# Fold of a fused attention and mixture kernel in another order, and the late rows' transpose ahead of expert 1's traffic

## The chip, the core and the metric

The kernel runs on one core of one Trainium2 chip. TensorE (PE) multiplies, VectorE (DVE), ScalarE (ACT) and GpSimd (POOL) do the rest, and SyncE (SP) issues most of the DMAs. The metric is device time in microseconds (us) of one execution; the median of three runs of the kernel before is 903.72 us (902.86 to 906.01).

## The reference

Three stages follow one another, all in float32:

```python
# 1: linear attention with a decaying state, batch 4, 8 heads, 768 steps, 48 wide
for t in range(S):
    cur = einsum('bhd,bhe->bhde', u * k[t], v[t])
    y[t] = einsum('bhd,bhde->bhe', r[t], state + cur)
    state = w[t] * state + einsum('bhd,bhe->bhde', k[t], v[t])
# 2: a bilinear layer on 3072 tokens, d_model 384, d_ff 1024
x = ((x @ w1) * (x @ w2)) @ w3 @ w_out
# 3: eight experts, the two best of each token, weighted
logits = x @ w_gate + log1p(exp(x @ w_noise)) * noise
out[mask] += top2_w * (relu(x[mask] @ e1[e]) @ e2[e])
```

## The kernel before

**Numbers.** Every large product runs as three passes on TensorE (`mm3`, L179 to L182): an operand is a high part in the PE's own float32 format plus a low part, the remainder, and the passes are high by high, high by low, low by high. The parts are made by `split` (L136) or, for the weights that the host hands over as 64-bit words, by `cvt` and `flush` (L142 to L171): ACT pulls the top 16 bits out (`top`, L151), DVE joins them with the middle bits (`cvz`, L164), ACT casts the high part (L166), DVE subtracts for the low part (L171). The weights come in through DMAs on SP's queue into seven buffers `rawf`.

**Stages.** (1) *Fold*, up to about 66 us: the product w3 times w_out is formed on the chip, widened by 16 gate columns (w_out times w_gate and w_noise). Step `u` of the loop at L529 converts one piece of w_out (`cv_wo`, `u < 8`) and one of w3 (`cv_w3`, `u < 16`), multiplies the piece converted three steps before (`mm_w3`, 12 matmuls of 400 columns), turns the new w_out piece over on PE (`wo_T`, L397) and multiplies the turned piece of the step before with the gate weights (`gate_cols`, `gate_split`). After `wo_T`, ACT copies the turned piece out of PSUM (`woT`, L402). `warm_up` puts matmuls on a constant tile among these. (2) *Groups*, up to about 467 us: twelve groups of two chunks of 128 tokens; the attention of later chunks is spread among the products of earlier ones. (3) *Experts*, eight, each in two halves: four tiles of 128 rows, then two of 128 and one of 32. Rows are gathered by POOL (`gather`), stored by SP to a DRAM table (`store_first` for expert 0, `turn` for the others), and read back through a transposing DMA on SP (`turn_first`, `turn`) into `XTx`; `tr` splits `XTx` into `XTh` on ACT and `XTl` on DVE, `mm1` and `mm2` multiply. For expert 0 the last tiles' rows (tiles 5 and 6, the late rows) are known last.

**What sets the order.** DVE's instructions run in the order in which the code is written. PE and ACT are ordered by the tile scheduler, ACT and some of PE in program order where the code pins it (`act.on`, `keep_in_program_order`). SP and POOL work their DMAs off in order; an SP entry that waits holds all behind it. Within the fold, the steps that prepare attention chunks 0 to 2 (`STEPS`, L377), the loads of their inputs and the loads and conversions of w1 and w2 (quarters, `load_w`, `cv_w`) are hung at slots by tables (`WHEN`, `WLD`, `WCV`, `LDA`); step `u` runs at its end all that stands in slots `u - 24` to `u - 23`. `WHEN[j][i]` is the slot of step `i` of chunk `j`.

Of the kernel before, what the change touches and what calls it, by code (L numbers as in the profile page):

```python
# [20 lines left out]
DM, FF, E = 384, 1024, 8  # L21
# [50 lines left out]
def tile_kernel(ctx: ExitStack, tc: tile.TileContext, dt, nat, w3t, wout, w1, w2, e1, e2, cf, ci, out):  # L72
    nc = tc.nc
    pe, act, dve, pool, sp = nc.tensor, nc.scalar, nc.vector, nc.gpsimd, nc.sync
# [13 lines left out]
    act = Pinned()  # L88

    def f(ap):  # L90
        return ap.bitcast(F32)
# [7 lines left out]
    cft = const.tile([P, CFW], F32, name="cft")  # L99
    cit = const.tile([P, CIW], I32, name="cit")  # L100

    def c(n):
        o, w = CF[n]
        return cft[:, o:o + w]
# [16 lines left out]
    trib = const.tile([P, P], BF16, name="trib")  # L121
# [14 lines left out]
    def split(h, l, src, on=None):  # L136
        act.copy(out=h, in_=src)
        (on or dve).tensor_tensor(out=l, in0=src, in1=f(h), op=OP.subtract)
# [3 lines left out]
    def cvt(rw, n, h, l, o=0, post=None):  # L142

        t = TOP[0][:, :n]
        TOP.append(TOP.pop(0))
        top = rw.bitcast(BF16)[:, 4 * o + 4:4 * o + 4 * n + 4].rearrange("p (n t) -> p n t", t=4)[:, :, 0]
        mid = rw[:, 2 * o + 1:2 * o + 2 * n + 1].rearrange("p (n t) -> p n t", t=2)[:, :, 0]  # L150
        act.activation(out=t.bitcast(F16).rearrange("p (n t) -> p n t", t=2)[:, :, 1], in_=top, func=AF.Copy)  # L151
        z = cvp.tile([P, 512], I32, name="cvz")[:, :n]
        if post == "z":
            dve.scalar_tensor_tensor(z, mid, 13, t, op0=OP.logical_shift_right, op1=OP.bitwise_or)
            return z.bitcast(F32)
        flush(1)
        CQ.append((mid, t, z, h, l, post))

    def flush(n=2):
        for _ in range(n):  # L160
            low, LQ[:] = LQ[:], []
            while CQ:
                mid, t, z, h, l, post = CQ.pop()
                dve.scalar_tensor_tensor(z, mid, 13, t, op0=OP.logical_shift_right, op1=OP.bitwise_or)  # L164
                x = z.bitcast(F32)
                act.copy(out=h, in_=x)  # L166
                LQ.append((h, l, x))
                if post:
                    post(x)
            for h, l, x in low:  # L170
                dve.tensor_tensor(out=l, in0=x, in1=f(h), op=OP.subtract)  # L171

    def load64(rw, src):

        n = src.shape[-1]
        sp.dma_start(out=rw.bitcast(U16)[:, 1:4 * n + 1], in_=src.bitcast(U16))
        return rw[:, :2 * n + 2]
# [205 lines left out]
    rawx, w3s, xo_, R1 = {}, {}, {}, {}  # L383
# [3 lines left out]
    def ld_raw(n=1):  # L387
        for _ in range(n):
            if order:
                k, u = order.pop(0)  # L390
                rawx[k, u] = load64(raws.tile([P, 1026], I32, name="rawf"),
                                    wout[u] if k == "o" else w3t[u // 8, u % 8])

    def cv_wo(j):
        cvt(rawx["o", j], DM, woh[:, j, :DM], wol[:, j, :DM], post=lambda x: xo_.__setitem__(j, x))

    def wo_T(j):  # L397
        bank = PB[4 + j % 2]
        for kb in range(3):
            pe.transpose(bank[:, P * kb:P * kb + P], xo_[j][:, kb * P:kb * P + P], ident)  # L400
        xo_[j] = fold.tile([P, DM], F32, name="woT")
        act.copy(out=xo_[j], in_=bank[:, :DM])  # L402

    def gate_cols(j):
        g = bK[:, 256 + 32 * j:272 + 32 * j]
# [3 lines left out]
    def gate_split(j):  # L409
        split(woh[:, j, DM:], wol[:, j, DM:], bK[:, 256 + 32 * j:272 + 32 * j])  # L410

    def cv_w3(u):
        w3s[u] = [fold.tile([P, 512], F32R, name=x, bufs=3) for x in ("w3h", "w3l")]
        cvt(rawx["3", u], 512, *w3s[u])
# [17 lines left out]
    def piece(m, fp, i):  # L432
        r = R1[m, fp]
        return (r[i], 0) if isinstance(r, list) else (r, 384 * i)
# [4 lines left out]
        cvt(rw, 384, (WAh, WBh)[m][:, sl], (WAl, WBl)[m][:, sl], o)  # L439

    def cv_early():
        for i in range(2):
            rw, o = piece(1, 0, i)
            EZ.append(cvt(rw, 384, None, None, o, "z"))
# [16 lines left out]
    def at(slot, fn, *a):  # L461
        todo.setdefault(slot, []).append((fn, a))

    def run_todo(lo, hi):
        for slot in sorted(x for x in todo if lo <= x < hi):
            for fn, a in todo.pop(slot):
                fn(*a)

    WHEN = {0: (-13, -12, -14, -13, -14, -21, -18, -17, -17, -20, -19, -16, -14, 0),
# [5 lines left out]
    LATE = (6, 6, 0, 1, 1, -6, -4, -3, -2, -5, -3, -2, -1, -2)  # L475
    JT = 5
    WLD = {(0, 0): -16, (0, 1): -14, (1, 0): -13, (1, 1): -11, (0, 2): -8, (1, 2): -6, (0, 3): 1, (1, 3): 3}
    WCV = {(0, 0): -10, (0, 1): -9, (1, 1): -4, (0, 2): -1, (1, 2): 2.65, (0, 3): 4.1, (1, 3): 6.01}
    WSP = (-5, -2, 2.6, 2.61)
    LDA = (-24, -22, -20, -17, -18)  # L480

    at(-23, lambda: sp.dma_start(out=cft[:, ca:], in_=cf[:, ca:]))
    at(-20, lambda: pool.tensor_copy(out=trib, in_=c("tri")))
    for slot, fn, a in zip(LDA, (load_dt, load_na, load_dt, load_na), (0, 0, 1, 1)):
        at(slot, fn, a)
    at(LDA[4], lambda: sp.dma_start(out=cit, in_=ci))
    at(-8, cv_early)
    at(-5, cv_late)
    for fb in range(4):
        at(WSP[fb], split_w1, fb)  # L490
    for k, slot in WCV.items():
        for i in range(2):
            if slot != -9:
                at(slot, cv_w, *k, i)
    for k, slot in WLD.items():
        at(slot, load_w, *k)
    for i, fn in enumerate(STEPS):
        for j in range(NCH):
            late = 3 if j == NCH - 1 and i == 1 else 0
            at(WHEN[j][i] if j in WHEN else 6 * j - 14 + LATE[i] - late, fn, j)  # L500
    for i in range(2):
        at(-9, cv_w, 0, 1, i)
    at(-3, flush)
    at(-3, flush, 1)
    for slot in (0.1, 2.55, 2.9, 3, 5, 5.3, 6.02, 6.04):
        at(slot, flush, 1)

    ca = CF["u"][0]
    sp.dma_start(out=cft[:, :ca], in_=cf[:, :ca])
    ld_raw(6)  # L510
    warm = fold.tile([P, 512], BF16, name="warm", bufs=1)
    dve.memset(warm, 1.0)

    def warm_up(n):
        for _ in range(n):
            tc.keep_in_program_order(pe.matmul(PB[6], warm[:, :P], warm, start=True, stop=True))
# [12 lines left out]
    for u in range(19):  # L529
        if u < 8:  # L530
            cv_wo(u)
            ld_raw()
        if u < 16:
            cv_w3(u)
            ld_raw()
        elif u == 16:
            flush()
        if u > 2:
            mm_w3(u - 3)
        if 0 < u < 9:  # L540
            gate_cols(u - 1)
            gate_split(u - 1)
        if u < 8:
            wo_T(u)
        if u < 2:
            warm_up(3)
        act.on = u >= 15
        run_todo(u - 24, u - 23)

    flush()  # L550
    foldx.close()
# [223 lines left out]
    def load_e(e, m, i):  # L775
        if m == 0 and e:
            rw = EP["b"].tile([P, 1536], F32, name="raww", bufs=2)
        else:
            rw = rawp.tile([P, 1538], F32, name="raw2", tag="raw64")[:, :1536]
        RW[e, m, i] = rw  # L780
        tc.keep_in_program_order(sp.dma_start(out=rw, in_=(e1, e2)[m][e, :, 1536 * i:1536 * i + 1536]))
# [57 lines left out]
    def rows_of(j):  # L839
        return TPT if j < NT - 1 else TPL  # L840
# [10 lines left out]
    def turn(e, hf, mid=lambda: None):  # L851

        for j in range(TA) if hf == 0 else range(TA, NT):
            tc.keep_in_program_order(sp.dma_start(
                out=rows[e % 2, 2 * TPT * j:2 * TPT * j + 2 * rows_of(j)].rearrange("(p t) d -> p (t d)", t=2),
                in_=XG[e, j][:rows_of(j)]))
        mid()
        a = 2 * hf * NAB[0]
        s = slice(a, a + 2 * NAB[hf])
        tc.keep_in_program_order(sp.dma_start_transpose(out=XT["x", hf].bitcast(U16), in_=rows[e % 2, s]))  # L860
# [56 lines left out]
    def need(e, hf, r, rows=NROW):  # L917
        load_idx(e, hf, r)
        for j in range(TA) if hf == 0 else range(TA, NT):
            gather(e, j, rows)  # L920
# [54 lines left out]
    for g in range(NGRP):  # L975
# [10 lines left out]
        for i in range(12):  # L986
# [11 lines left out]
            k = SPG * g + i  # L998
# [47 lines left out]
    for j in range(TA):  # L1046
        mm2(0, j)
        if j == 0:
            need(1, 0, 0)
            for jj in (NT - 2, NT - 1):  # L1050
                store_first(jj)
            turn_first(NT - 2, CAP)
            load_e(1, 0, 0)
            load_e(1, 0, 1)
        if j == TA - 2:
            tr(0, 1)
    need(1, 1, 0)

    def load_w2():
        load_e(1, 1, 0)  # L1060
        load_e(1, 1, 1)

    for ff in range(8):
        mm1(1, ff)
    turn(1, 0)
    for i, j in enumerate((TA, NT - 1, *range(TA + 1, NT - 1))):
        mm2(0, j)
        split_e(1, 0, i)
# [132 lines left out]
```

## Time and profile before

| what | value |
|---|---|
| median of three runs | 903.72 us |
| the profiled execution, whole | 909.49 us |
| its span, first to last instruction | 907.7 us |
| PE busy | 882.4 us (97%) |
| DVE, ACT, POOL busy | 491.6, 436.3, 242.9 us |
| PE's share of the chain that ended last | 41%, DMA 1%, issue 2% |

A page of the profile lists busy time by engine, by slice of the span and by line; queries of the trace give the same for any stretch, list instructions in order of time with the idle time of the engine before each and what ended it, and sum who waited for whom. Times in them count from the span's start. Busy PE can hold inefficiency: a matmul's row lasts longer than the distance to the next one's start, because they are pipelined.

### The profile page before, as it was taken

Reading aid. Unit: us, or ns where it says so; the run is one execution under the profiler, and the core shown is the slowest. Engines: PE = TensorE matmul, PEld = TensorE weight load, DVE = VectorE, ACT = ScalarE, POOL = GpSimd, SP = SyncE. Lnnn points to the kernel's source line nnn. Section 1 sums busy time; section 2 is a strip of 40 time slices with the busy share of each in tenths; the row PEclk is TensorE's granted clock in tenths of the full one; section 3 lists DMA queues with packets and bytes.
Section 4 is the critical chain, followed back from the end, with each engine's and each line's share of the span. In section 5 each row is a group of like instructions: output and inputs, shape, how many; then the busy total and the mean of one; then the engine's idle time right before and its main releaser. Section 6 shows DMA issues by size and latency. Waiting matters only on the chain. (4 is left out here: it accounts for less than half of the span.)

```text
span 907.7 us, 17628 instructions
## 1 busy us (share of the span) xinstructions
PE 882.4 (97%) x7010; PEld 816.1 (90%) x7010; DVE 491.6 (54%) x1208; ACT 436.3 (48%) x883; POOL 242.9 (27%) x216
## 2 busy tenths in 40 slices
PE   8899999999999999999998999999999999999994
PEld 6789799999999999999988989899998989989894
DVE  5899766756666657655472453443434334353430
ACT  7787666555546547544552443433334343433320
POOL 1200010231231231132334443316061341603122
PEclk9999999999999999999999999999999999999997
DMA  9963479474575654515145986829276482934112
GB/s 352 409 232 129 130 99 262 130 196 142 144 216 139 178 134 128 146 44 167 36 114 108 256 249 173 204 73 222 62 214 143 133 213 65 229 76 108 18 21 38
DMA packets 123581, 139.18 MB, mean 153 GB/s; under 512 B 74592, under 2 KB 103264, under 8 KB 123488
## 3 DMA queue, kind: packets, MB, share of 16 engines
q1 hardware_dynamic: 99952, 109.58, 41.3%
q0 software_dynamic: 12160, 19.72, 11.2%
q10 hardware_dynamic: 11376, 8.65, 3.3%
q8 instruction: 57, 0.93, 0.4%
q14 instruction: 36, 0.29, 0.1%
HBM read 88.12 MB, written 36.04 MB: 137 GB/s over the span
## 5 line engine op out<-in xcount | busy, mean ns | idle before, releaser
L908 POOL DMA_INDIRECT out<-ye,ti x49 | 77.4, 1579 | 235.5 <-ACT ye L898 215.3
L180 PE MATMUL pb<-XTh,WAh 128*128 128x512 f32 (+1 forms) x384 | 134.2, 350 | 3.0 <-ACT XTh L865 2.3
L181 PE MATMUL pb<-XTl,WAh 128*128 128x512 f32 (+1 forms) x384 | 133.0, 347 | 0.0
L182 PE MATMUL pb<-XTh,WAl 128*128 128x512 f32 (+1 forms) x384 | 131.8, 347 | 0.0
L180 PE MATMUL pb<-WBh,HH 128*128 128x384 f32 x384 | 130.2, 339 | 0.0
L181 PE MATMUL pb<-WBl,HH 128*128 128x384 f32 x384 | 129.3, 337 | 0.0
L182 PE MATMUL pb<-WBh,HH 128*128 128x384 f32 x384 | 129.3, 337 | 0.0
L881 DVE SCALAR_TENSOR_TENSOR HH<-pb,HH 128x256 fp32r<-128x256 f32 (+1 forms) x128 | 71.3, 557 | 87.2 <-ACT HH L880 79.9
L880 ACT ACTIVATE HH<-pb 128x256 fp32r<-128x256 f32 (+1 forms) x128 | 62.8, 491 | 115.2 <-PE pb L182 108.2
L898 ACT ACTIVATE ye<-pb,ti 128x384 f32<-128x384 f32 x42 | 24.4, 581 | 134.0 <-PE pb L182 108.4
L725 POOL DMA_INDIRECT slots<-g_sc,g_si x48 | 51.9, 1081 | 136.9 <-DVE g_si L724 71.9
L180 PEld LDWEIGHTS pb<-XTh,WAh 128*128 128x128 f32 x384 | 72.7, 189 | 15.1 <-DVE HH L881 4.0
L180 PE MATMUL pb<-xh,WAh 128*128 128x256 f32 x288 | 82.0, 285 | 0.3 <-ACT xh L86 0.3
L180 PE MATMUL pb<-xh,WBh 128*128 128x256 f32 x288 | 81.5, 283 | 0.0
L181 PE MATMUL pb<-xl,WAh 128*128 128x256 f32 x288 | 81.0, 282 | 0.2 <-DVE xl L337 0.2
L181 PE MATMUL pb<-xl,WBh 128*128 128x256 f32 x288 | 81.0, 281 | 0.0
L182 PE MATMUL pb<-xh,WAl 128*128 128x256 f32 x288 | 81.0, 282 | 0.0
L182 PE MATMUL pb<-xh,WBl 128*128 128x256 f32 x288 | 81.0, 281 | 0.0
L181 PEld LDWEIGHTS pb<-XTl,WAh 128*128 128x128 f32 x384 | 72.8, 190 | 8.8 <-DVE XTl L866 0.3
L182 PEld LDWEIGHTS pb<-XTh,WAl 128*128 128x128 f32 x384 | 72.3, 189 | 8.8 <-DVE WAl L791 0.2
L180 PEld LDWEIGHTS pb<-WBh,HH 128*128 128x128 f32 x384 | 72.1, 188 | 5.0 <-ACT WAh L788 3.8
L241 POOL TENSOR_TENSOR rku<-nrk 128x384 f32<-128x384 f32 x21 | 21.6, 1028 | 198.7 <-DVE cc L248 83.5
(194 smaller groups left out, 2063.5 us busy)
## 6 DMA issues: line engine op xcount, KB each, us to landing
dtc<-dt SPq DMA_DIRECT2D x24, 772.0 KB
raw<-e SPq DMA_DIRECT2D x18, 768.0 KB
raww<-e SPq DMA_DIRECT2D x14, 768.0 KB
nrk<-nat SPq DMA_DIRECT2D x24, 384.0 KB
expert_rows<-xg SPq DMA_DIRECT2D x45, 192.0 KB
rawf<-w3t SPq DMA_DIRECT2D x16, 512.0 KB
nv<-nat SPq DMA_DIRECT2D x24, 256.0 KB
out<-zeros SPq DMA_DIRECT2D x9, 576.0 KB
```

What stands on the lines that cost most here:

```text
L180: pin(pe.matmul(o, wh, xh, start=start, stop=False))
L181: pe.matmul(o, wh, xl, start=False, stop=False)
L182: pe.matmul(o, wl, xh, start=False, stop=stop)
L241: on.tensor_tensor(out=t, in0=RK[j][:, :DM], in1=RK[j][:, DM:], op=OP.mult)
L725: ins = pool.indirect_dma_start(out=table, out_offset=bass.IndirectOffsetOnAxis(ap=si[:, i, k:k + 1], axis=0), in_=SC[:, i, k, :], in_offs ...
L880: act.activation(out=Hh[hf][:, ff], in_=bank[:, :n], func=AF.Relu)
L881: dve.scalar_tensor_tensor(Hl[hf][:, ff], bank[:, :n], 0.0, f(Hh[hf][:, ff]), op0=OP.max, op1=OP.subtract)
L898: act.activation(out=y[:n], in_=bank[:n], func=AF.Copy, scale=wt)
L908: ins = pool.indirect_dma_start(out=out, out_offset=bass.IndirectOffsetOnAxis(ap=ti(e, j)[:, 0:1], axis=0), in_=y[:n], in_offset=None, com ...
```

## The change

Five edits. The line numbers after the first edits grow by some: 402 becomes 403 and 405, 407 becomes 410, 516 becomes 518, 822 becomes 827, 829 becomes 834, 800 becomes 805, 781 becomes 786, 854 becomes 859, 860 becomes 865, 908 becomes 913.

1. Front of the fold: the first w_out piece is loaded ahead of the constants `cft` (identity and gate weights); six warm-up matmuls stand behind the first gate product instead of three behind the second turned piece.
2. The cast of the first w_out piece's high part and the copies of six of the eight turned pieces go from ACT to DVE.
3. Each step of the fold runs its slots in two halves, one ahead of its matmuls and one at its end, and the tables have new slots for chunks 0 to 2, for the loads and conversions of w1 and w2 and for the constants. `cv_early` first empties the pending conversions.
4. The late rows of expert 0 are stored and transposed before expert 1's index lists are fetched and its rows gathered.
5. The load of expert 1's first weights moves from right behind that transpose to behind the stores of expert 1's first half.

```diff
-                act.copy(out=h, in_=x)
+                (act.copy if xo_ else dve.tensor_copy)(out=h, in_=x)
...
         xo_[j] = fold.tile([P, DM], F32, name="woT")
-        act.copy(out=xo_[j], in_=bank[:, :DM])
+        if j < 6:
+            dve.tensor_copy(out=xo_[j], in_=bank[:, :DM])
+        else:
+            act.copy(out=xo_[j], in_=bank[:, :DM])
...
     def cv_early():
+        flush(1)
...
-    WHEN = {0: (-13, -12, -14, -13, -14, -21, -18, -17, -17, -20, -19, -16, -14, 0),
+    WHEN = {0: (-12.5, -11.5, -13.5, -12.5, -15.0, -20.6, -17.5, -17.05, -17.0, -20.0, -19.0, -16.5, -12.6, 0),
...
+    ld_raw()
     sp.dma_start(out=cft[:, :ca], in_=cf[:, :ca])
-    ld_raw(6)
+    ld_raw(5)
...
+        run_todo(u - 24, u - 23.5)
         if u > 2:
             mm_w3(u - 3)
         if 0 < u < 9:
             gate_cols(u - 1)
             gate_split(u - 1)
+        if u == 1:
+            warm_up(6)
         if u < 8:
             wo_T(u)
-        if u < 2:
+        if u == 0:
             warm_up(3)
         act.on = u >= 15
-        run_todo(u - 24, u - 23)
+        run_todo(u - 23.5, u - 23)
...
         if j == 0:
-            need(1, 0, 0)
             for jj in (NT - 2, NT - 1):
                 store_first(jj)
             turn_first(NT - 2, CAP)
-            load_e(1, 0, 0)
-            load_e(1, 0, 1)
+            need(1, 0, 0)
...
+    def load_w1():
+        load_e(1, 0, 0)
+        load_e(1, 0, 1)
...
-    turn(1, 0)
+    turn(1, 0, load_w1)
```

`need(e, hf, r)` issues the index lists of half `hf` of expert `e` on SP (`ti<-slots`) and their gathers on POOL; `turn(e, hf, mid)` stores the gathered rows, calls `mid` and issues the transpose.

**VectorE at the fold's start.** `cvz` is a joined piece, `woT` a turned one, `WBh` and `WBl` the parts of w_out, `w3h` and `w3l` those of w3. Before:

```order
L164 SCALAR_TENSOR_TENSOR cvz<-rawf,top_110 128x384
L164 SCALAR_TENSOR_TENSOR cvz<-rawf,top_111 128x512
L171 TENSOR_TENSOR WBl<-cvz,WBh 128x384
L164 SCALAR_TENSOR_TENSOR cvz<-rawf,top_110 128x384
L171 TENSOR_TENSOR w3l<-cvz,w3h 128x512
L138 TENSOR_TENSOR WBl<-pb_73,WBh 128x16
```

and of the change:

```order
L164 SCALAR_TENSOR_TENSOR cvz<-rawf,top_110 128x384
L166 CAST WBh<-cvz 128x384
L403 COPY woT<-pb_70 128x384
L164 SCALAR_TENSOR_TENSOR cvz<-rawf,top_111 128x512
L171 TENSOR_TENSOR WBl<-cvz,WBh 128x384
L164 SCALAR_TENSOR_TENSOR cvz<-rawf,top_110 128x384
L171 TENSOR_TENSOR w3l<-cvz,w3h 128x512
L138 TENSOR_TENSOR WBl<-pb_73,WBh 128x16
L403 COPY woT<-pb_71 128x384
```

The cast and the turned pieces' copies have come into DVE's list.

**ScalarE at the fold's start.** Before:

```order
L151 ACTIVATE top_110<-rawf 128x384
L166 CAST WBh<-cvz 128x384
L402 COPY woT<-pb_70 128x384
L151 ACTIVATE top_111<-rawf 128x512
L137 CAST WBh<-pb_73 128x16
L151 ACTIVATE top_110<-rawf 128x384
L166 CAST w3h<-cvz 128x512
```

and of the change:

```order
L151 ACTIVATE top_110<-rawf 128x384
L151 ACTIVATE top_111<-rawf 128x512
L137 CAST WBh<-pb_73 128x16
L151 ACTIVATE top_110<-rawf 128x384
L166 CAST w3h<-cvz 128x512
```

The first w3 piece's `top` follows the first w_out piece's at once.

**SyncE at the late rows.** `tf` and `ti` are index lists of expert 0 and 1, `raww` expert 1's first weights, `XTx_..` 128x3x320 the late rows' transpose. Before:

```order
L808 DMA tf<-slots 32x2
L800 DMA ti_6379<-slots 128x8
L1098 TENSOR_LOAD rounds
L1098 ISA x2
L822 DMA expert_rows<-xg 128x768
L822 DMA expert_rows<-xg 32x768
L829 DMA_TRANSPOSE XTx_6344<-expert_rows 128x3x320
L781 DMA raww<-e 128x1536 x2
L800 DMA ti_6483<-slots 128x4
L800 DMA ti_6483<-slots 32x2
L854 DMA expert_rows<-xg 128x768 x4
L860 DMA_TRANSPOSE XTx_5806<-expert_rows 128x3x1024
```

and of the change:

```order
L813 DMA tf<-slots 32x2
L1105 TENSOR_LOAD rounds
L1105 ISA x2
L827 DMA expert_rows<-xg 128x768
L827 DMA expert_rows<-xg 32x768
L834 DMA_TRANSPOSE XTx_6347<-expert_rows 128x3x320
L805 DMA ti_6385<-slots 128x8
L805 DMA ti_6482<-slots 128x4
L805 DMA ti_6482<-slots 32x2
L859 DMA expert_rows<-xg 128x768 x4
L786 DMA raww<-e 128x1536 x2
L865 DMA_TRANSPOSE XTx_5809<-expert_rows 128x3x1024
```

The first list `ti` has gone from ahead of the late rows' stores to behind their transpose, and the weights from ahead of expert 1's four stores to behind them, right ahead of expert 1's transpose. On POOL, where expert 1's four gathers stood ahead of expert 0's first output, that output now stands first. Behind the fold, ACT's and DVE's orders are those of before.

## Rows read from the trace of the kernel before

**Rows 1.** Busy by stretch: length, engines' busy us (instructions), PEclk, DMA share, GB/s.

```profile
10.00:70.00 60.00, 56.55 (x438) 49.61 (x436) 50.91 (x98) 47.77 (x105) 4.93 (x5) 1.00 0.86 331
165.00:480.00 315.00, 314.40 (x3238) 300.43 (x3237) 200.98 (x626) 172.88 (x358) 86.76 (x83) 1.00 0.50 138
```

**Rows 2.** PE's waits, 10 to 70 us: us in total, times, longest.

```profile
PE pb L181 <- DVE WBl L138: 0.9, 1, 0.9
PE pb L180 <- ACT w3h L166: 0.8, 2, 0.4
...
PE pb L180 <- ACT xh L86: 0.3, 1, 0.3
```

**Rows 3.** PE by time, the start: start, us, line, tiles, [idle before <-releaser].

```profile
5.67 0.55 PE L400 MATMUL pb<-cft,cvz 128*128 128x128 f32 x3 [0.53 <-DVE cvz L164]
6.79 0.84 PE L407 MATMUL pb<-cft,woT 128*128 128x16 f32 x6
8.88 0.63 PE L180 MATMUL pb<-WBh,w3h 128*128 128x400 f32 x2 [1.25 <-ACT w3h L166]
```

**Rows 4.** PE by time, expert 0's second half.

```profile
499.06 0.55 PE L180 MATMUL pb<-XTh,WAh 128*128 128x288 f32 x1 [2.27 <-ACT XTh L865]
503.25 0.29 PE L180 MATMUL pb<-XTh,WAh 128*128 128x288 f32 x1
510.39 0.34 PE L180 MATMUL pb<-WBh,HH 128*128 128x384 f32 x1
```

**Rows 5.** ACT by time, the late rows and expert 1.

```profile
498.58 1.10 ACT L865 CAST XTh<-XTx 128x288 fp32r<-128x288 f32 x3 [5.33 <-DMA XTx<-expert_rows]
517.44 1.65 ACT L865 CAST XTh<-XTx 128x512 fp32r<-128x512 f32 x3
```

**Rows 6.** Busy by stretch there, PEclk third from the end.

```profile
499.00:501.00 2.00, 1.94 (x7) 1.68 (x8) 1.20 (x3) 1.15 (x4) 0.00 (x0) 0.54 1.04 366
490.00:497.00 7.00, 6.79 (x40) 6.47 (x38) 0.00 (x0) 0.58 (x1) 5.60 (x5) 1.00 0.95 156
```

**Rows 7.** SP's queue by time, the late rows and expert 1.

```profile
491.95 1.27 SPq L829 DMA_TRANSPOSE XTx<-expert_rows  x1
493.26 1.05 SPq L781 DMA_DIRECT2D raww<-e  x2
494.36 0.90 SPq L800 DMA_DIRECT2D ti<-slots  x2
506.31 4.18 SPq L860 DMA_TRANSPOSE XTx<-expert_rows  x1
...
544.66 1.48 SPq L860 DMA_TRANSPOSE XTx<-expert_rows  x1
```

**Rows 8.** Busy by stretch after the transpose issued at 544.66 us.

```profile
544.60:545.60 1.00, 1.00 (x10) 1.00 (x9) 0.52 (x2) 0.19 (x2) 0.00 (x0) 1.00 0.00 0
548.60:549.60 1.00, 1.00 (x8) 1.00 (x7) 0.24 (x2) 0.00 (x0) 0.00 (x0) 1.00 0.00 0
```

**Rows 9.** POOL by time, a gather of expert 1.

```profile
504.70 1.01 POOL L848 DMA_INDIRECT xg<-x_rows,ti  x1 [7.89 <-DMA ti<-slots]
```

**Rows 10.** ACT by time, the fold.

```profile
4.39 0.64 ACT L151 ACTIVATE top<-rawf 128x384 f16<-128x384 bf16 x1 [2.36 <-DMA rawf<-wout]
6.26 0.48 ACT L402 COPY woT<-pb 128x384 f32<-128x384 f32 x1
8.24 0.59 ACT L166 CAST w3h<-cvz 128x512 fp32r<-128x512 f32 x1
18.12 0.17 ACT L137 CAST WBh<-pb 128x16 fp32r<-128x16 f32 x1 [1.18 <-PE pb L407]
```

**Rows 11.** DVE by time, the fold.

```profile
5.06 0.56 DVE L164 SCALAR_TENSOR_TENSOR cvz<-rawf,top 128x384 int32<-128x384 int32 x1 [3.65 <-ACT top L151]
48.85 0.55 DVE L337 TENSOR_TENSOR xl<-pb,xh 128x384 fp32r<-128x384 f32 x1
```

**Rows 12.** DVE's waits, 5 to 67 us.

```profile
DVE cvz L164 <- ACT top L151: 12.9, 11, 3.7
```

More of the change, by code (lines that the diff above doesn't have):

```diff
@@ L476, in tile_kernel @@
     JT = 5
-    WLD = {(0, 0): -16, (0, 1): -14, (1, 0): -13, (1, 1): -11, (0, 2): -8, (1, 2): -6, (0, 3): 1, (1, 3): 3}
-    WCV = {(0, 0): -10, (0, 1): -9, (1, 1): -4, (0, 2): -1, (1, 2): 2.65, (0, 3): 4.1, (1, 3): 6.01}
+    WLD = {(0, 0): -18.0, (0, 1): -12.7, (1, 0): -12.5, (1, 1): -10.5, (0, 2): -7.5, (1, 2): -6.5, (0, 3): 1, (1, 3): 3}
+    WCV = {(0, 0): -8.3, (0, 1): -8.0, (1, 1): -3.9, (0, 2): -1, (1, 2): 2.65, (0, 3): 4.1, (1, 3): 6.01}
     WSP = (-5, -2, 2.6, 2.61)
-    LDA = (-24, -22, -20, -17, -18)
-    at(-23, lambda: sp.dma_start(out=cft[:, ca:], in_=cf[:, ca:]))
-    at(-20, lambda: pool.tensor_copy(out=trib, in_=c("tri")))
+    LDA = (-23.8, -22.5, -18.5, -16.5, -17.3)
+    at(-22.5, lambda: sp.dma_start(out=cft[:, ca:], in_=cf[:, ca:]))
+    at(-19.5, lambda: pool.tensor_copy(out=trib, in_=c("tri")))
     for slot, fn, a in zip(LDA, (load_dt, load_na, load_dt, load_na), (0, 0, 1, 1)):
@@ L486, in tile_kernel @@
     at(LDA[4], lambda: sp.dma_start(out=cit, in_=ci))
-    at(-8, cv_early)
+    at(-5.5, cv_early)
     at(-5, cv_late)
@@ L492, in tile_kernel @@
         for i in range(2):
-            if slot != -9:
-                at(slot, cv_w, *k, i)
+            at(slot, cv_w, *k, i)
     for k, slot in WLD.items():
@@ L500, in tile_kernel @@
             at(WHEN[j][i] if j in WHEN else 6 * j - 14 + LATE[i] - late, fn, j)
-    for i in range(2):
-        at(-9, cv_w, 0, 1, i)
     at(-3, flush)
```

4 rows, old and new, of the table WHEN are left out of this document.

## The prediction

> **What bounds the kernel now.** I read the busy time by stretch first, then PE's waits, then the three places that these point to in order of time. From 165 to 480 us PE stands idle 0.60 of 315 us, so the groups are bound by PE and no edit touches them [rows 1]. From 10 to 70 us PE idles 3.45 us (60 less 56.55), in short waits for the parts that ACT and DVE make of the weights [rows 1, 2]. Ahead of that stands the start, where the first w3 product waits until 8.88 us [rows 3]. The largest single hole is elsewhere: at 499.06 us the late rows' product waited 2.27 us for `XTh`, and ACT had waited for the transposing DMA [rows 4, 5]. In the stretch behind it the granted clock is 0.54, so it ran between the two levels, mostly at 1.2 GHz instead of 2.4 [rows 6]. The reader is to see that the DMA is an issue in that one place alone, and conversions in the fold.
>
> **The late rows, edits 4 and 5.** The price of the hole has two parts. Idle: 2.27 us. Clock: the half has eight blocks of nine passes, 72 matmuls, from 499.06 to 510.39 us, 11.33 us; the last 54 of them run from 503.25 to 510.39, 7.14 us, 0.132 us each; 72 at that rate are 9.52, so 1.81 us went to the start at half clock [rows 4]. Together 4.08 us. The transpose was issued at 491.95 and ACT began at 498.58, 6.63 us later [rows 5, 7]. To close the hole ACT must begin 2.27 us earlier, so 4.36 us are allowed. What does it take alone? A larger transpose (576 half rows against 320) was issued at 544.66; the DMA engines are idle until 545.60 and again from 548.60, so it took at most 3.94 us, some 3.0 of it data [rows 7, 8]. In between 490 and 497 the engines are 0.95 busy at 156 GB/s, with five POOL transfers beside it and 1.5 MB of `raww` behind it [rows 6, 7]. The change takes expert 1's gathers and weights out of that stretch and leaves one output. I take it to land in time: -4.08 us. Bounds: 0 if it takes as long as before, -4.08 if not.
>
> What is late next: expert 1's index list, gathers and stores come later, and its weights (two transfers of 768 KB) now stand right ahead of its transpose. That transpose was issued at 506.31 and ACT took it up at 517.44 without a wait [rows 5, 7]; everything is now due 4.08 us sooner, at 513.36. The weights take 1.57 MB at 331 GB/s, 4.75 us [rows 1]; the transpose of 1024 half rows by proportion 3.0 times 1024/576, 5.3 us of data. If its issue stays at 506.31 that ends at 516.4, 3.0 us late. Against this: the list no longer lies behind `raww` (the second list did, and its gather waited to 504.70 [rows 7, 9]), and the weights' data fall into the dead first microsecond of the transpose. So 0 to 3.0 us given back; I take 0.5, near the low end, because PE takes the first `XTh` only once the rest of expert 0's product is done. Net -3.6.
>
> **The start, edits 1 and 2.** The first w_out piece goes from SP's second place to its first, 0.3 to 0.45 us by the distance of SP's issues (an estimate; ACT's first row waited for that DMA alone [rows 10]). `top` ends 0.64 us after 3.94, DVE joins, then casts and copies. A copy of 128x384 out of PSUM on DVE isn't in the trace; the nearest row is the subtraction of that size from PSUM, 0.55 us, against ACT's 0.48 [rows 10, 11]; I take 0.55, with 0.3 and 0.7 as the ends. So the turned piece is ready at about 6.35 instead of 6.74. ACT, free of cast and copy, makes the first w3 piece's `top` directly behind the first one instead of at the copy's end, so its `w3h`, 0.59 us from 8.24 before, ends some 0.3 us sooner [rows 10]. The six warm-up matmuls now fill a stretch in which PE stood idle 1.25 us [rows 3], and three no longer stand behind the second turned piece. I take -0.4 us; bounds -0.8 and +0.5.
>
> **The rest of the fold, edits 2 and 3.** ACT loses six copies of 0.48 and a cast of about the same, 3.4 us; DVE gains seven of 0.55, 3.85 us. What hides them: DVE waits for ACT's `top` 12.9 us between 5 and 67, of which 3.7 are the start, so 9.2 us are open [rows 12], and those waits shrink as ACT is relieved. ACT's own stall at 18.12, 1.18 us for the gate product with the next piece's `top` queued behind it, is of the sort that the new order takes out (there the gate's cast stands behind that `top`) [rows 10]. Of PE's waits I count the 0.8 for `w3h` and the 0.3 for `xh` as gone (the last attention product now stands ahead of w1's conversions), and half of the 0.9 for `WBl`: -1.6 us [rows 2]. The moved chunk steps issue the same instructions and DMAs; the w1 quarter loaded earlier stands ahead of w3 pieces that are used later. Bounds: -3.45, all of the idle, and +3.85, if DVE's list simply becomes that much longer.
>
> **Sum.** -3.6, -0.4 and -1.6 are -5.6 us. The profiled execution took 909.49 us, 907.7 in the span and 1.8 around it; with the change 903.9. It lies 5.77 us over the median of the runs, 903.72, so for the median 898.1 us.
>
> **The rivals.**
> *The transpose still shares its engines.* POOL's first output, an accumulating write, now runs beside the transpose in place of the gathers; if that is enough to stretch it to 6 us, the hole stays over 1.6 us wide and with it the clock's fall. For it: 0.95 busy at 156 GB/s, far below the 331 of the fold, so it is not bytes that fill the engines [rows 1, 6]. Against it: five transfers against one. It leaves -0.5 there, and with the fold 903.72 - 0.5 - 2.0 = 901.2. The Trainium skill (DMA: Bandwidth & Descriptors, Queues, rings and completion order) says that each DMA engine serves its queues in turn, packet by packet, and one queue's descriptors in ring order; by that rule the weights behind the transpose took nothing from it, and only what POOL sends counts. The row of 490 to 497 fits it, without proving it.
> *The fold gives nothing.* What ACT saves DVE pays; PE's waits change their names. For it: DVE is 50.9 busy of those 60 us, ACT 47.8 [rows 1]. Then 903.72 - 3.6 = 900.1.
> *Expert 1 late.* The whole 3.0 us come back, and the clock falls again for 1.8: -4.08 + 4.8, with the fold's -2.0: 902.4. By the same section's ring order the transpose starts behind 1.5 MB of weights; the list that waited behind them before agrees [rows 7, 9].
> *Slower: DVE becomes the fold's bound.* DVE works in written order. If each of six copies waits for PE as ACT's gate cast did (1.18) and none of DVE's old waits shrink, its list is 3.85 + 7.1 = 10.9 us longer; half of that, 5.5, with the late rows' -3.6, is 905.6. It decides from the point where the fold ends 3.6 us later than now.
>
> **How the numbers follow.** Forecast 898.1: 0.57. Fold gives nothing, 900.1: 0.16. Transpose still slow, 901.2: 0.14. Expert 1 late, 902.4: 0.05. DVE the bound, 905.6: 0.08. About 0.3%, 2.7 us, is what a measurement here can tell from no change, so faster means under 901.0 and slower over 906.4. Faster: 0.56 of the forecast, 0.12 and 0.06 of the next two, 0.74. Slower: the upper half of the last case, which reaches to 911 if all of the 10.9 come, 0.04. Same: the rest, 0.22. The range goes down to 895.0 (start -0.8, the idle of the fold nearly all gone, nothing given back) and up to 903.0, which leaves the slower rival and a part of the late ones out. The likeliest case alone reaches from 896 to 900.5.
>
> **What would show it.** Right: PE's first w3 product at about 8.5 us; the fold's last product ends 2 us earlier; idle from 10 to 70 us under 2.5; ahead of the late rows' product no wait over 0.5 us, and a granted clock of 1.00 in the stretch behind it; expert 1's `XTh` waits at most a microsecond on ACT and PE not at all. Wrong: a wait of PE for `XTh` at either place, the clock at 0.5 there, or DVE without idle from 10 to 35 us while PE waits for `woT` or `cvz`.

## The result and the profile after

| | median us | lowest to highest | runs | profiled execution (span) |
|---|---|---|---|---|
| before | 903.72 | 902.71 to 908.13 | 11 | 909.49 (907.7) |
| after | 910.58 | 906.04 to 913.86 | 11 | 907.63 (905.8) |

The ratio after to before is 1.0062, with a 95% interval from 1.0044 to 1.0081. On 903.72 us that is 5.6 us slower (4.0 to 7.3); the two medians lie 6.9 apart. The forecast was 898.1, from 895.0 to 903.0. It was wrong in sign.

The two profiled executions compare the other way round: that of before lies above every timed run of its kernel, that of after in the lower part of its own. So the spans must not be subtracted; only places can be compared.

**What went as forecast: the late rows.** ACT by time, after (start, us, line, tiles, idle before and its releaser): expert 0's third output cast, the late rows' cast, and expert 1's:

```profile
490.22 0.58 ACT L903 ACTIVATE ye<-pb,tf 128x384 f32<-128x384 f32 x1 [3.58 <-PE pb L182]
490.70 1.09 ACT L870 CAST XTh<-XTx 128x288 fp32r<-128x288 f32 x3
516.99 1.66 ACT L870 CAST XTh<-XTx 128x512 fp32r<-128x512 f32 x3 [6.14 <-DMA XTx<-expert_rows]
```

The late rows' cast has no wait in front of it, where before ACT waited 5.33 us for the transposing DMA [rows 5]. PE does not wait there either. The transpose itself got faster too, as the prediction had it: where ACT waited for it in profiles with edit 4, the cast began 3.2 to 3.5 us behind its issue (six profiles), in the old order 4.2 to 6.8 us behind it (eight). The last row is the new fault: before, expert 1's cast followed without a wait [rows 5]. What PE lost by it, in PE's waits from 480 to 530 us (us in total, times, longest), and by time:

```profile
PE pb L180 <- ACT XTh L870: 3.8, 1, 3.8
PE pb L181 <- DVE XTl L871: 0.2, 1, 0.2
```

```profile
517.66 0.49 PE L180 MATMUL pb<-XTh,WAh 128*128 128x512 f32 x1 [3.77 <-ACT XTh L870]
519.00 0.63 PE L180 MATMUL pb<-XTh,WAh 128*128 128x512 f32 x1
522.84 0.40 PE L181 MATMUL pb<-XTl,WAh 128*128 128x512 f32 x1
```

A pass's row lasts 0.63 us at 519.00 and 0.40 at 522.84. Busy by stretch (PEclk third from the end) says why, and shows the fold and the groups beside it:

```profile
10.00:70.00 60.00, 57.20 (x443) 50.15 (x443) 53.58 (x105) 45.19 (x100) 5.26 (x5) 1.00 0.85 324
165.00:480.00 315.00, 315.00 (x3245) 302.38 (x3245) 203.69 (x630) 174.57 (x361) 87.06 (x83) 1.00 0.49 138
518.90:522.30 3.40, 3.40 (x9) 2.64 (x9) 2.46 (x4) 1.68 (x3) 1.57 (x1) 0.50 1.06 352
```

The clock fell to 1.2 GHz behind the wait, 3.40 us long, which cost half of that, 1.7 us. With 3.8 and 0.2 the turn from expert 0 to expert 1 lost 5.7 us in this execution. What came late there, by SP's queue and POOL in order of time:

```profile
486.15 1.27 SPq L834 DMA_TRANSPOSE XTx<-expert_rows  x1
...
498.38 0.95 SPq L786 DMA_DIRECT2D raww<-e  x2
503.30 8.65 SPq L865 DMA_TRANSPOSE XTx<-expert_rows  x1
```

```profile
490.24 0.99 POOL L853 DMA_INDIRECT xg<-x_rows,ti  x1 [5.36 <-DMA ti<-slots]
```

The late rows' transpose went out 5.8 us earlier than before, expert 1's only 3.0 us earlier [rows 7]. Of both, 2.45 us are the place of the whole turn, whose third output cast stands at 490.22 here and stood at 492.67 before:

```profile
492.67 0.58 ACT L898 ACTIVATE ye<-pb,tf 128x384 f32<-128x384 f32 x1 [3.58 <-issue]
```

So against PE's work expert 1's transpose gained only 0.6 us: its list, and with it the first gather, now waits behind the late rows. Its issue alone occupied SP for 8.65 us instead of 4.18, and ACT could start only 13.7 us after it began (503.30 to 516.99).

**The fold.** PE's idle time from 10 to 70 us went from 3.45 to 2.80 us, not to the 1.85 that the forecast comes to. The last w3 product began at 65.78 us against 65.82 before, not 2 us earlier. PE's waits there, after:

```profile
PE pb L181 <- DVE WBl L138: 0.9, 2, 0.6
PE pb L261 <- DVE WBl L138: 0.5, 1, 0.5
PE pb L400 <- DVE cvz L164: 0.5, 1, 0.5
PE pb L180 <- ACT w3h L166: 0.4, 2, 0.3
```

Half of the wait for `w3h` and that for `xh` are gone, but new ones for `WBl` and `cvz` stand in their place [rows 2]. DVE's waits for ACT's `top` halved, from 12.9 to 6.3 us [rows 12], and DVE now waits for PE once:

```profile
DVE cvz L164 <- ACT top L151: 6.3, 6, 3.1
...
DVE woT L403 <- PE pb L400: 1.1, 1, 1.1
```

The start gained nothing that can be seen; PE's first w3 product:

```profile
9.31 0.45 PE L180 MATMUL pb<-WBh,w3h 128*128 128x400 f32 x1
```

It was at 8.88 us before [rows 3], and the forecast said 8.5. In a second profile of before it stood at 9.16.

### The profile page after: what moved, and what is told of

Same layout as the page of the kernel before. It is cut to its first block, busy times and chain, and to the rows that moved or that the text cites. A ratio compares the mean times of both kernels' runs of the same rounds, so it can differ in the third digit from the quotient of the medians.

```text
span 905.8 us, 17633 instructions
## 1 busy us (share of the span) xinstructions
PE 882.7 (97%) x7013; PEld 817.0 (90%) x7013; DVE 495.6 (55%) x1215; ACT 434.2 (48%) x876; POOL 242.3 (27%) x216
## 3 DMA queue, kind: packets, MB, share of 16 engines
q10 hardware_dynamic: 11376, 8.65, 2.9%
## 4 chain that ended last, share of the span: by engine, by line
PE 89%; DVE 5%; DMA 2%; ACT 2%; issue 1%; POOL 0%; POOLq 0%; ACTq 0%; DVEq 0%
PE pb L180 27%; PE pb L181 26%; PE pb L182 26%; PE pb L330 4%; PE pb L261 3%; DMA XTx<-expert_rows 2%; PE pb L293 1%; PE pb L908 1%; DMA rawf<-wout 1%; PE pb L518 1%; DVE cvz L164 1%; DVE am L266 0%; PE pb L410 0%; DVE fg L208 0%; POOL out L913 0%
## 5 line engine op out<-in xcount | busy, mean ns | idle before, releaser
L796 DVE TENSOR_TENSOR WAl<-raww,WAh 128x768 fp32r<-128x768 f32 x28 | 26.7, 958 | 87.8 <-ACT WAh L793 87.8
```

Of the source, the lines that this page charges most:

```text
L796: dve.tensor_tensor(out=l, in0=src, in1=f(h), op=OP.subtract)
```

## The experiments

Each job ran on one chip, and the kernel before took 906.07, 913.43, 912.83, 912.88 and 905.64 us median in the five jobs. So only ratios to the before of the same job are compared. "The turn" is the transition from expert 0 to expert 1.

### First job: which half of the change

**fold_only**: edits 4 and 5 undone, the turn as before.

```diff
         if j == 0:
+            need(1, 0, 0)
             ...
             turn_first(NT - 2, CAP)
-            need(1, 0, 0)
+            load_e(1, 0, 0)
+            load_e(1, 0, 1)
-    turn(1, 0, load_w1)
+    turn(1, 0)
```

> The kernel after with edits 4 and 5 undone: the fold and the start are new, the turn from expert 0 to expert 1 is as before. Theory TURN (the loss is made where expert 1's transpose lands late, 3.8 us of wait and a stretch at half clock; the fold gains about 2 us): 900.5 to 903.5 us, no wait of PE for expert 1's XTh over 0.5 us. Theory FOLD (the new order of the fold loses in most runs, and the one profiled execution does not show it): 908 to 911 us.

Measured 904.11 us, ratio 0.9989 (0.9970 to 1.0007). TURN holds. What the fold gave is 1.0 us, between 2.7 less and 0.6 more. Its turn, SP and then ACT by time:

```profile
490.54 1.27 SPq L834 DMA_TRANSPOSE XTx<-expert_rows  x1
...
505.03 6.17 SPq L865 DMA_TRANSPOSE XTx<-expert_rows  x1
```

```profile
493.76 0.58 ACT L903 ACTIVATE ye<-pb,tf 128x384 f32<-128x384 f32 x1 [3.58 <-PE pb L182]
497.35 1.10 ACT L870 CAST XTh<-XTx 128x288 fp32r<-128x288 f32 x3 [3.01 <-DMA XTx<-expert_rows]
```

Here the late rows' transpose, in its old place, was issued 3.2 us ahead of the output cast at 493.76, and PE waited for nothing. In the profile that the prediction was made from it was issued at 491.95 [rows 7], 0.7 us ahead of that cast (492.67), and PE waited 2.27 us. The old order does not have the hole in every run.

**late_only**: the kernel before with edits 4 and 5, the same lines the other way.

> The kernel before with edits 4 and 5 alone: late rows' store and transpose first, expert 1's weights right ahead of its transpose; the fold is as before. TURN: 909 to 913 us, with a wait of PE for expert 1's XTh of 3 us or more. FOLD: 900 to 904 us, about 4 us under the kernel before if the hole at the late rows is in its usual run, none if not.

Measured 911.20 us, ratio 1.0072 (1.0045 to 1.0099): the whole loss, without the new fold. PE's waits and SP:

```profile
PE pb L180 <- ACT XTh L865: 6.9, 1, 6.9
```

```profile
510.74 9.09 SPq L860 DMA_TRANSPOSE XTx<-expert_rows  x1
```

**w_early**: the weights behind the index list again; edit 4 stays.

```diff
             turn_first(NT - 2, CAP)
             need(1, 0, 0)
+            load_e(1, 0, 0)
+            load_e(1, 0, 1)
-    turn(1, 0, load_w1)
+    turn(1, 0)
```

> The kernel after with edit 5 alone undone: expert 1's first weights are issued right behind its index list again, long before its transpose; edit 4 stays. RING (the weights stand ahead of the transpose in SP's queue and that makes it late): 898 to 903 us, PE waits under 0.5 us for expert 1's XTh, the transpose lands within 8 us of its issue. POOL (the outputs and gathers that POOL sends beside it stretch it): 907 to 911 us, the transpose takes 10 us or more from issue to landing. FOLD: 908 to 911 with no such wait.

Measured 904.35 us, ratio 0.9985 (0.9968 to 1.0003); against after that is 0.8% by the two ratios. POOL as the only cause falls: POOL's gathers and outputs are all still there. SP and ACT:

```profile
507.01 3.47 SPq L865 DMA_TRANSPOSE XTx<-expert_rows  x1
```

```profile
492.95 0.58 ACT L903 ACTIVATE ye<-pb,tf 128x384 f32<-128x384 f32 x1 [3.58 <-PE pb L182]
...
513.88 1.66 ACT L870 CAST XTh<-XTx 128x512 fp32r<-128x512 f32 x3 [0.31 <-DMA XTx<-expert_rows]
```

6.9 us from issue to cast, half of after's 13.7.

**w_behind**: the weights right behind the transpose instead of ahead of it.

```diff
-    turn(1, 0, load_w1)
+    turn(1, 0)
+    load_w1()
```

> The kernel after with the two weight loads moved behind expert 1's transpose instead of ahead of it. RING: the transpose lands within 8 us of its issue and PE does not wait for XTh; but the weights now land 5 us or more later and ACT's first WAh cast can wait for them: 901 to 907 us. POOL: the transpose still takes 10 us or more, 908 to 912 us.

Measured 909.94 us, ratio 1.0058 (1.0031 to 1.0086). Both expectations missed a part: the transpose's issue took 4.62 us again and ACT did not wait for it, but ACT waited for the weights, with the transpose's cast queued behind. ACT by time:

```profile
516.27 0.83 ACT L793 CAST WAh<-raww 128x768 fp32r<-128x768 f32 x1 [3.60 <-DMA raww<-e]
...
518.21 1.65 ACT L870 CAST XTh<-XTx 128x512 fp32r<-128x512 f32 x3
```

PE waited 1.0 us for `XTh` and 2.2 us for `XTl`. In these two profiles, after's and this one, the order in SP's queue chose which of the two was late.

### Second job: was the hole usual, and what stretches the transpose

**before_again**: unchanged.

> The kernel before, unchanged, for a second profile and the granted clock of its timed runs. USUAL (the hole at the late rows is part of its usual run): a wait of PE for the late rows' XTh of 1.5 us or more and a stretch at 0.5 behind it, a mean clock of 0.993 or less in most runs, profile and median close together. RARE (the one profiled execution was an unusual one): no such wait over 0.5 us, a mean clock of 0.995 in most runs, as in the kernel whose fold alone is new.

914.13 us on a chip where before itself took 913.43. PE's waits at the turn:

```profile
PE pb L180 <- ACT XTh L865: 1.9, 2, 1.3
```

A hole again at the late rows, but of 1.3 us (PE's product at 500.78), and no stretch at half clock behind it; the other 0.6 us is expert 1's. The runs' mean clock went from 0.985 to 0.996. That is neither USUAL nor RARE: the hole comes and goes in size.

**late4**: the kernel before with edit 4 alone, that is w_early with the old fold.

> The kernel before with edit 4 alone: late rows' store and transpose first, then expert 1's list, then its weights where they were. USUAL: 4 us less than the kernel before, 900 to 902 us. RARE: within 1.5 us of it. In both no wait of PE for the late rows, and for expert 1 under 0.5 us.

912.58 us, ratio 0.9988 (0.9961 to 1.0014). Edit 4 alone gave 1.1 us, between 3.6 less and 1.3 more; the forecast for it, 3.6 with the giveback, is at the very end of that. In its profile PE waited 2.6 us for expert 1's `XTh` all the same: the wait had moved on. No load stood ahead of this transpose, and yet ACT's cast began 11.2 us behind its issue, not 6.9:

```profile
507.28 6.35 SPq L860 DMA_TRANSPOSE XTx<-expert_rows  x1
```

```profile
518.44 1.66 ACT L865 CAST XTh<-XTx 128x512 fp32r<-128x512 f32 x3 [4.90 <-DMA XTx<-expert_rows]
```

**w_half**: one of the two loads early, one right ahead of the transpose.

```diff
             need(1, 0, 0)
+            load_e(1, 0, 0)
     def load_w1():
-        load_e(1, 0, 0)
         load_e(1, 0, 1)
```

> The kernel after with the first of expert 1's two weight loads early again (behind its index list) and the second alone right ahead of its transpose. QUEUE (the weights still in flight ahead of it delay the transpose, by what is left of them): the landing moves from 13 to about 10 us after the issue, PE waits 0.5 to 2 us for XTh, 905 to 908 us. ISSUE (the place alone does it, whatever its size): as in the kernel after, 909 to 912 us.

914.69 us, ratio 1.0016 (0.9985 to 1.0047), and PE waited 2.8 us, with the cast 10.9 us behind the issue. ISSUE's 909 to 912 us, 0.6% and more over before, lie above the interval; QUEUE's time and way fit, its wait of at most 2 us does not. Run again below.

**pool_later**: the second list and its three gathers behind the transpose's issue.

```diff
-    need(1, 1, 0)
     ...
     turn(1, 0, load_w1)
+    need(1, 1, 0)
```

> The kernel after with the three gathers of expert 1's second part, and their list, moved behind the issue of expert 1's first transpose; the weights stay right ahead of it. POOL (gathers beside the weights and the transpose stretch both): the weights land some 3 us sooner and PE's wait for XTh falls below 1.5 us, 904 to 908 us. QUEUE: the transpose still lands 11 us or more after its issue and PE waits 2.5 us or more, 908 to 912 us.

919.12 us, ratio 1.0054 (1.0019 to 1.0090). PE no longer waits for the first `XTh`; the cast began 9.4 us after the issue. By this one profile the gathers take part. The time holds neither theory off, for expert 1's second part now came late:

```profile
PE pb L180 <- DVE HH L886: 7.2, 2, 6.7
```

### Third job: another place for the weights, and the fold's parts

**w_pocket** and **pocket_oldfold**: the weights at some 472 us, with the new fold and with the old.

```diff
     turn_first(TA, TPT * (TA + 1))
+    load_e(1, 0, 0)
+    load_e(1, 0, 1)
     ...
-    turn(1, 0, load_w1)
+    turn(1, 0)
```

> The kernel after with expert 1's two weight loads issued at some 472 us, right behind the transpose of expert 0's fifth tile, where the DMA engines of the kernel after are 0.03 to 0.27 busy; edit 4 and the fold stay. TRAFFIC (what is in flight between 495 and 515 us makes the transpose late, weights and POOL's transfers alike; 1.5 MB less of it helps): no wait of PE for either XTh, turn as in the kernel with early weights (32.2 us from the third output cast to expert 1's first HH) or less, 0.2 to 0.5% under before. PLACE (the loads only had to stand ahead of the stores): no better than that kernel, 0.0 to 0.2% under before.

> The same transition with the fold and the start of the kernel before; against the run before it, the fold alone differs, with the turn out of the way. FOLD GAINS (as forecast): 1.5 to 2.5 us slower than that run. FOLD GIVES NOTHING: within 1 us of it, and ACT's landmark at 113 us no later.

915.31 and 914.52 us, ratios 1.0015 (0.9983 to 1.0046) and 1.0021 (0.9987 to 1.0055). The place is no better than w_early's, so TRAFFIC's forecast missed. But it is no clean test of what is in flight at the transpose: in pocket_oldfold's profile expert 1's transpose had a short way (512.79 to 520.57, 7.8 us) and a late issue, 16.8 us behind the third output cast. The late rows' own list `tf`, which now stands behind the weights in SP's queue, went out 8.4 us ahead of that cast, in late4 10.2 us ahead. w_pocket's profiled execution took 925.17 us, and its turn is not read here. As to the fold, the old one's median is 0.8 us the lower, its ratio 0.0006 the higher: no gain is shown, but the two intervals leave room for FOLD GAINS.

**front_only**, edit 1 alone, and **copies_only**, edit 2 alone.

```diff
+    ld_raw()
     sp.dma_start(out=cft[:, :ca], in_=cf[:, :ca])
-    ld_raw(6)
+    ld_raw(5)
     ...
+        if u == 1:
+            warm_up(6)
     ...
-        if u < 2:
+        if u == 0:
             warm_up(3)
```

```diff
-                act.copy(out=h, in_=x)
+                (act.copy if xo_ else dve.tensor_copy)(out=h, in_=x)
     ...
+        if j < 6:
+            dve.tensor_copy(out=xo_[j], in_=bank[:, :DM])
+        else:
+            act.copy(out=xo_[j], in_=bank[:, :DM])
```

> The kernel before with edit 1 alone: the first w_out load in front of the constants, six warm-up matmuls behind the first gate product in place of three behind the second turned piece. Forecast: 0.4 us less, with 0.8 less and 0.5 more as ends, and PE's first w3 product at about 8.6 us. If the start hides nothing: within 0.2 us of before, and the product at 8.9 us.

> The kernel before with edit 2 alone: the first cast and six copies on DVE, the old slots. DVE BOUND: DVE's list grows by 3.9 us of work and by waits for PE, the fold ends 2 us or more later, 905.5 to 909 where before is 903.7. RELIEF: ACT's stalls go and the fold ends 0.5 to 1.5 us sooner.

front_only: 910.78 us, 0.9979 (0.9954 to 1.0003), with the first w3 product at 9.32 us, not 8.6. The interval just includes no change, and its profile shows no place for a gain. copies_only: 912.66 us, 1.0003 (0.9972 to 1.0034). That leaves room for DVE BOUND only up to 3.1 us, and for RELIEF up to 2.6; the times show neither. The execution that was profiled took 917.38, 4.7 us over the median, and there the fold's last w3 product began at 72.22 us, with the granted clock at 0.50 from 10 to 16 us and DVE waiting 2.2 us for PE at `woT`.

### Fourth and fifth job: doses, and the edits apart

**load5**: the kernel before with edit 5 alone.

```diff
             turn_first(NT - 2, CAP)
-            load_e(1, 0, 0)
-            load_e(1, 0, 1)
     ...
-    turn(1, 0)
+    turn(1, 0, load_w1)
```

> The kernel before with edit 5 alone: expert 1's two weight loads leave their place behind the late rows' transpose and stand right ahead of expert 1's. EDIT 5 ALONE HURTS: 0.4 to 0.8% over before, the transpose lands 11 us or more after its issue, PE waits 2 us or more for its XTh. IT NEEDS EDIT 4 (with the old order the list and the gathers go first, so the weights meet less traffic): within 0.2% of before, landing within 9 us.

912.21 us, ratio 0.9992 (0.9963 to 1.0022): edit 5 alone costs nothing. SP and ACT:

```profile
502.77 6.77 SPq L860 DMA_TRANSPOSE XTx<-expert_rows  x1
```

```profile
494.68 0.58 ACT L898 ACTIVATE ye<-pb,tf 128x384 f32<-128x384 f32 x1 [3.65 <-PE pb L182]
...
517.43 1.65 ACT L865 CAST XTh<-XTx 128x512 fp32r<-128x512 f32 x3
```

The transpose is issued 8.1 us after the output cast at 494.68; in after it was 13.1 (490.22 to 503.30). The late rows go as in before here, and PE waited 1.4 us for them.

**after_again**, **w_half2** and **w_early2**: two, one and no load ahead of the transpose, on one chip. The first is the kernel after, the others are w_half and w_early.

> The kernel after, unchanged, as the dose of two loads ahead of expert 1's transpose, on one chip with doses one and none, and a second profile of it. QUEUE: the transpose lands some 13 us after its issue again, 0.4 to 0.8% over before. If the lateness was peculiar to the first profile: landing within 9 us.

> One load ahead of the transpose, the other early. QUEUE: between the other two doses, 0.1 to 0.5% over before, landing at about 10 us. ISSUE (the place, not the size): as with two.

> No load ahead of the transpose, both early: 0.3% under to 0.1% over before, landing within 8 us of the issue, no wait of PE over 0.5 us, in both theories.

| loads ahead | ratio | interval | from the transpose's issue to ACT's cast |
|---|---|---|---|
| 2 | 1.0062 | 1.0033 to 1.0091 | 13.0 us (511.01 to 524.05) |
| 1 | 1.0018 | 0.9996 to 1.0040 | 11.5 us (507.54 to 519.02) |
| 0 | 1.0004 | 0.9978 to 1.0031 | 7.9 us (512.56 to 520.45) |

In these three profiles it grows with the load, and after's ratio came out the same on another chip. One profile each is little for the lower steps: late4, with no load ahead, had 11.2 us, and w_half, with one, 10.9. PE's wait for the cast, of two loads, and of one:

```profile
PE pb L180 <- ACT XTh L870: 4.8, 1, 4.8
```

```profile
PE pb L180 <- ACT XTh L870: 1.7, 1, 1.7
```

**need_first**: the kernel after with edit 4 alone undone.

```diff
         if j == 0:
+            need(1, 0, 0)
             for jj in (NT - 2, NT - 1):
                 store_first(jj)
             turn_first(NT - 2, CAP)
-            need(1, 0, 0)
```

> The kernel after with edit 4 alone undone: expert 1's index list and first gathers go ahead of the late rows' store and transpose again, its weights stay right ahead of its transpose, the fold is new. BOTH NEEDED (edit 4 issues the transpose some 5 us later, edit 5 lengthens its way by some 5 us; either alone fits): within 0.3% of before, the transpose issued within 10 us of the third output cast of expert 0 and landed within 20. EDIT 5 ALONE (the run of it in the kernel before was lucky): 0.4 to 0.8% over before, landing 25 us or more behind that cast.

905.91 us, ratio 1.0009 (0.9978 to 1.0040): BOTH NEEDED on the time. The execution that was profiled took 911.13 us, 5.2 over its median, and shows how it can still go wrong. SP and ACT:

```profile
498.64 13.23 SPq L865 DMA_TRANSPOSE XTx<-expert_rows  x1
```

```profile
520.42 1.66 ACT L870 CAST XTh<-XTx 128x512 fp32r<-128x512 f32 x3 [6.28 <-DMA XTx<-expert_rows]
```

Issued only 5.1 us after the output cast (493.52), and yet 21.8 us on its way; the landing in 20 us was missed, and PE waited 3.9 us.

**tables_only**: edit 3 alone, the slots.

```diff
-    WLD = {(0, 0): -16, (0, 1): -14, (1, 0): -13, ...
+    WLD = {(0, 0): -18.0, (0, 1): -12.7, (1, 0): -12.5, ...
     ...
+        run_todo(u - 24, u - 23.5)
     ...
-        run_todo(u - 24, u - 23)
+        run_todo(u - 23.5, u - 23)
```

> The kernel before with edit 3 alone: the new slots of the fold and the half steps, the copies and the cast still on ACT, the start as before. The prediction took most of the fold's 1.6 us from this order: 0.1 to 0.25% under before. If the order only renames the waits: within 0.1%. If it needs the copies on DVE: 0.1 to 0.4% over before, with PE's waits for WBl and cvz grown.

904.90 us, ratio 0.9990 (0.9963 to 1.0017). Nothing that can be told from no change, nor from the 1.6 us that the prediction took. Its profile from 10 to 70 and from 36 to 40 us:

```profile
10.00:70.00 60.00, 58.26 (x433) 52.09 (x432) 49.34 (x95) 45.08 (x100) 4.61 (x5) 0.94 0.82 311
36.00:40.00 4.00, 4.00 (x14) 3.29 (x15) 3.21 (x6) 3.24 (x9) 0.00 (x0) 0.50 1.03 411
```

PE idles 1.74 us instead of 3.45 [rows 1], but the granted clock fell to 1.2 GHz on the way, and the one cannot be had apart from the other here.

No version beat the kernel before beyond its interval. Without its fifth edit (w_early) the change loses nothing that can be told, and gains nothing that can be told.

## Why the prediction was wrong

The four cases of edits 4 and 5 side by side, ratios to before:

| | edit 5 not made | edit 5 made |
|---|---|---|
| edit 4 not made | 1 (old fold), 0.9989 (new) | 0.9992 (old), 1.0009 (new) |
| edit 4 made | 0.9988 (old), 0.9985 and 1.0004 (new) | 1.0072 (old), 1.0062 and 1.0062 (new) |

Neither edit alone shows a loss (the intervals end at 1.0003 to 1.0040); together they cost 0.6 to 0.7%, with either fold. That is the result, and the times show it. How it comes about is read from single profiles, of the issue of expert 1's transpose and its way (from the issue to ACT's cast). PE can take expert 1's cast without a wait if it starts within 23.0 us of expert 0's third output cast: in after it started 26.8 us behind that cast (490.22 to 516.99) and PE waited 3.8. Edit 4 puts the list behind the late rows' transpose, and POOL's first gather waits for it; with it, expert 1's transpose was issued 12.3 to 17.1 us after the output cast (ten profiles, w_pocket's pair aside). With neither edit it was 11.3 to 15.1 (six), so edit 4 alone does not make it much later. Edit 5 without edit 4 brings the issue to 5.1 and 8.1, where no weights stand ahead of list and stores. But edit 5 makes the way longer, 13.0 to 13.7 us with edit 4 (after, after_again, late_only), where w_early's took 6.9 and 7.9 and late4's 11.2. What edit 5 gains at the issue pays for its longer way, and is lost once edit 4 is there as well: 14.1 and 6.9 are 21.0, in time (w_early); 8.1 and at most 14.7 are 22.8, in time (load5); 13.1 and 13.7 are 26.8, late (after). The one profile that does not fit this sum is need_first's, 5.1 and 21.8, taken 5.2 us above the median of its kernel.

Point by point.

- *The late rows, -4.08.* The hole closed as described, but in the timed runs it was not there to be won at that size. Edit 4 alone gave 1.1 us (late4), or nothing (w_early 904.35 against fold_only 904.11 on one chip). The step that failed is in the sum: the profiled execution lay 5.77 us above the median, and I carried these 5.77 along as a constant, as if they had nothing to do with the stall. But a stall that the timed runs lack cannot be taken off their median: fold_only, with the same turn, waits for nothing, and before_again waits 1.3 us at full clock. A mark in the profile says that it came from a slower chip than the times (last section). The hole goes with that mark: of the profiles with the late rows in their old order, four of five with the mark have a wait of PE there (2.3, 1.3, 1.4 and, in copies_only, 1.2 us), and none of the three without it (fold_only, tables_only, need_first). How much of the 5.77 is the chip and how much the hole is not shown.
- *The giveback, 0.5, bounds 0 to 3.0.* This term turned the sign: 5.7 us. I worked out 3.0 us from the bytes at full rate, which puts the end of the transpose 10.1 us behind its issue, and then chose near zero because "the weights' data fall into the dead first microsecond of the transpose". They did not: the weights went out at 498.38, among three gathers and two outputs of POOL that were issued from 497.25 to 502.93, and the transpose's way took 13.7 us, twice that of w_early. The step that failed here is the way: it was sized as if weights and transpose had the engines to themselves. The deadline was off as well, the other way: 513.36 came from ACT's start, and by the 23.0 us it was 515.7. The upper bound also lacked the clock's 1.7 us, although a rival had it.
- *Expert 1 late, 902.4, given 0.05.* This rival had the place and the mechanism, and with 4.8 nearly the price. It failed with the same step as the forecast, the 4.08 counted as won. Without it, 903.72 and 5.7 are 909.4; the waits of 4.8 and 6.9 us in the other two profiles of such a turn show that 3.8 was a mild one. By the Trainium skill (DMA: Bandwidth & Descriptors, Queues, rings and completion order) one queue's descriptors are taken in ring order on each DMA engine. w_behind agrees so far, since with the weights behind it the transpose's issue took 4.62 us again; when it landed cannot be read there, since ACT was held by the weights.
- *The start, -0.4.* Not seen: the product stands at 9.31 us, against 8.88 and 9.16 in two profiles of before.
- *The rest of the fold, -1.6.* With the start it was -2.0. By fold_only it is 1.0 less (2.7 less to 0.6 more). The traces show no gain: one and the same cast of `ph` on ACT, behind the fold, stands at 112.85 to 115.18 us in six profiles with the old fold, mean 113.9, and at 112.63 to 115.64 in eleven with the new, mean 114.5. The waits for `xh` and half of those for `w3h` that I counted as gone went, and others came. What the term left out is the clock. In six of the twelve profiles with the new tables (tables_only, fold_only, need_first, w_early2, pool_later, w_pocket) the granted clock fell to its lower level within 34 to 42 us, in none of the eight with the old ones; in three of those (load5, late_only, copies_only) it fell within 8 to 18 us. By the mean clock of 2 us stretches (an estimate) such a fall cost 1.7 us, in tables_only and copies_only (its first) 3.4. After itself has no fall, after waits of much the same size; what decides it stays open, and so does how often the timed runs had it. DVE did not become the bound in after: its waits for `top` shrank, as the prediction had it.

What stays open: how the engines share between the weights, POOL's transfers and the transpose. Queue order alone does not explain it (w_behind loses as well), nor do POOL's transfers alone (w_early keeps them and is in time). The amount in flight in those 20 us fits these and the doses, but not late4's 11.2 us without a load ahead; w_pocket, which was to test it, delayed the late rows' list as well.

## What to carry to other kernels

Before a stall is put into a sum, ask whether the timed runs have it: a profiled execution above all of the timed ones is a warning that its largest wait may be the difference. Where two edits draw on one slack, add up the path to the next deadline with both in it (issue, way, deadline): here neither showed a loss and the pair did. When a transfer is freed by moving others behind it, price the next transfer on the same path as carefully as the one freed.

## What the runs showed of the hardware

The issue of one and the same transpose, of 1024 half rows, held SP for 3.47 us in w_early and for 13.23 us in need_first. So the length of such a row is not a fixed cost of issuing.

The kernel before took 903.7 to 906.1 us in three jobs (that of the first table and two of the five) and 912.8 to 913.4 in three. All twelve profiles from the slower jobs have one small wait that the seven from the others lack, after's among them; in before_again, PE's waits from 440 to 487 us:

```profile
PE pb L672 <- DVE g_mb L655: 0.4, 1, 0.4
```

The profile that the prediction was made from has it too, 0.4 us ahead of 450.95. By this sign it came from a chip of the slower sort, and the times beside it, 903.72, from one of the faster.
